# Decode attention with cached keys and values: TensorE's value products as a loop, and the spreading mask in PSUM

## The chip, the cores and the metric

The kernel runs on one NeuronCore of a Trainium2 chip. A core has TensorE (matrix products, called PE in the profile, with its weight loads as PEld), VectorE (DVE), ScalarE (ACT), GpSimd (POOL) and SyncE (SP, which here only issues transfers), and 16 DMA engines that move data between HBM and the on-chip memory SBUF. TensorE writes to PSUM, which VectorE and ScalarE can also read. The engines run apart from one another and wait on semaphores.

The metric is the time of one execution in microseconds, as the median of several runs. All numbers below in us are from one profiled execution, unless the runs are named.

## The reference

One decode step of a transformer block with batch 4, width 512, 32 heads of 128, and 4096 cached positions, all in float32:

```python
mod = (_silu(c) @ w_mod).reshape(c.shape[0], 6, 1, -1)   # sa, ca, ga, sb, cb, gb
h = _layernorm(x) * (1 + ca) + sa
q = h @ wq                                               # 4 x 32 heads x 128
scores = einsum("bhqd,bhkd->bhqk", q, k_cache) * (Dh ** -0.5)
o = einsum("bhqk,bhkd->bhqd", softmax(scores), v_cache)
x = x + ga * (o @ wo)
h = _layernorm(x) * (1 + cb) + sb
x = x + gb * (silu(h @ w1) @ w2)
```

The two caches are 4 x 32 x 4096 x 128 floats each, 268 MB; together with the weights 567 MB are read once.

## The kernel before

The attention is cut into 32 tiles; tile `n` is one batch row and four heads. Its keys `k` (8.4 MB) and values `v` (8.4 MB) are loaded whole: partition `32 h + p` of `k` holds 128 consecutive positions of head `h`, 64 KB. There are two buffers for `k` (`kt[n % 2]`) and one for `v` (`vt`), so that the load of `v` for tile `n + 1` can be issued only when TensorE has read the values of tile `n`, and the load of `k` for tile `n + 2` stands behind it in SyncE's queue.

A tile's work, in `tile(n)` and `values(n)`:

- **Products with the query.** VectorE multiplies positions 0 to 47 by the query, which ScalarE has copied to PSUM (`qload`). GpSimd multiplies positions 48 to 127 in three pieces (`CUTS`).
- **Sums.** VectorE adds up the products along the 128 elements of a head (`scores`), first for positions 0 to 79 (`NA = 80`), later for 80 to 103 and 104 to 127.
- **Softmax in two halves.** `ownmax` takes the maximum of a head's 32 partitions, ScalarE takes the exponential of a half.
- **Spread.** `spread` writes the exponentials of a half into `pz`, once for each of four heads, multiplied by `mask`, a 128 x 4 table that is 1 where the partition belongs to the head and 0 elsewhere. So one TensorE product serves four heads. It is one VectorE instruction for a half: 320 elements in a partition for the first half and 192 for the second.
- **Value products.** `pv` multiplies `pz` by `v`, 20 products for the first half into one PSUM bank, 12 for the second into another, with one product for the sums of the exponentials (`fps`) between. VectorE and ScalarE join the halves into `o`, and four small products and a copy bring it into `oz`.

After tile 31 come the projection with `wo` (`regroup`, `project`), the layer norm and the two products with `w1` and `w2`; the loads of these weights stand behind the last `v` in SyncE's queue.

Instructions are recorded by the class `Plan` in program order; it works out which semaphores each must wait for, and leaves out a wait that an earlier one implies. Each engine then executes its own instructions in that order. TensorE's stream begins at a label of its own. Instructions recorded while `pl.loop` is set, which is so in `values(n)` for tiles 0 to 30, carry the tile and their place in it. Where `LOOP` is false they are written out one after the other, 37 products for each tile. Each float32 product shows in the profile as two matmuls and two weight loads.

Of the kernel before, what the change touches and what calls it, by code (L numbers as in the profile page):

```python
# [6 lines left out]
AF = mybir.ActivationFunctionType  # L7
# [1 line left out]
AX = mybir.AxisListType  # L9
ET = mybir.EngineType  # L10
PE = [ET.PE]
LOOP = False
SLOT = 16


# [25 lines left out]
class Plan:  # L41
# [108 lines left out]
    def run(self, end):  # L150
# [11 lines left out]
        with nc.body("pe_main", valid_engines=PE):  # L162
            done = False
            for o in self.ops:
                if o.eng != "PE":
                    continue
                if o.loop and LOOP:
                    if not done:
# [16 lines left out]
def build(nc, x, kc, vc, wq, wo, w1, w2, c, wm, out):  # L185
    P = 128
# [3 lines left out]
    G = 4  # L190
    W = P // G
    HP = 4
# [4 lines left out]
    JJ = 4  # L197
# [13 lines left out]
    def sb(name, *shape, at=None):  # L211
        size = 4
        for s in shape:
            size *= s
        if at is None:
            at = base[0]
            base[0] += -(-size // 32) * 32
            assert base[0] <= nc.sbuf_usable_end, (name, base[0])
        return nc.alloc_sbuf_tensor_at(name, [P, *shape], F32, offset=at)
# [10 lines left out]
    bank = [nc.alloc_psum_tensor(f"ps{i}", [P, 512], F32) for i in range(8)]  # L230
    dsem = {}

    def dma(dst, src, tag, eng="SP"):
        if tag not in dsem:
            dsem[tag] = nc.alloc_semaphore("d_" + tag)
        s = dsem[tag]
        e = pl.eng[eng]
        return pl.op(eng, lambda: e.dma_start(dst, src), [], [dst], sem=s)  # L238

    def dve(f, reads, writes):  # L240
        return pl.op("DVE", f, reads, writes)

    def act(f, reads, writes):
        return pl.op("ACT", f, reads, writes)
# [14 lines left out]
    def tt(eng, o, a, b, op=ALU.mult):  # L259
        e, q = (V, dve) if eng == "DVE" else (GP, pool)  # L260
        return q(lambda: e.tensor_tensor(o, a, b, op=op), [a, b], [o])  # L261
# [10 lines left out]
    def actv(o, a, fn, scale=1.0, bias=None, accum=None):  # L272
        kw = {"scale": scale}
        reads, writes = [a], [o]
        if not isinstance(scale, float):
            reads.append(scale)
        if bias is not None:
            kw["bias"] = bias
            if not isinstance(bias, float):
                reads.append(bias)  # L280
        if accum is not None:
            kw["accum_out"] = accum
            writes.append(accum)
        return act(lambda: A.activation(o, a, fn, **kw), reads, writes)  # L284

    def bc(a, dim, n):
        a = a.unsqueeze(dim)
        shape = list(a.shape)
        shape[dim] = n
        return a.to_broadcast(shape)  # L290
# [4 lines left out]
    mask = sb("mask", G)  # L295
# [71 lines left out]
    def vload(n, *cuts):  # L367
        t, b = divmod(n, B)
        src = vc[b, HP * t : HP * (t + 1)].rearrange("h (p j) d -> (h p) j d", p=W)
        cuts = cuts or (0, NJ)  # L370
        for i, (lo, hi) in enumerate(zip(cuts, cuts[1:])):
            tag = "C" if len(cuts) == 2 else f"v{i}"
            dma(vt[:, lo:hi, :], src[:, lo:hi, :], tag)
# [83 lines left out]
    def qexpand(t):  # L457
        j, g = divmod(t, G)
        ps = bank[2 + t % 2]
        for i in range(HP):  # L460
            mm(
                ps[W * i : W * (i + 1), :], mask[:, g : g + 1].to_broadcast([P, W]),
                E[:, HP * j + i, :, :].rearrange("p b d -> p (b d)"), True, True,
            )
        actv(qw[:, t, :], ps[:, :], AF.Copy)
# [10 lines left out]
    for t in range(1, NT):  # L476
        qexpand(t)
    vload(0)
    for i in (2, 3):
        dve(lambda i=i: V.memset(bank[i][:, :], 0.0), [], [bank[i][:, :]])  # L480

    ev = ea.rearrange("p (g j) -> p g j", j=JJ)
# [7 lines left out]
    def spread(lo, hi):  # L490
        g0, g1 = lo // JJ, hi // JJ
        w = pz[:, g0:g1, :, :]
        tt("DVE", w, bc(ev[:, g0:g1, :], 2, HP), bc(bc(mask[:, :], 1, g1 - g0), 3, JJ))

    def ownmax(h, src, col):
        rm = sc[:, col : col + 1]
# [16 lines left out]
    def tile(n):  # L513
        t, b = divmod(n, B)
        k = kt[n % 2]
        tt("DVE", k[:, :ND, :], k[:, :ND, :], bc(bank[n % 2][:, :Dh], 1, ND))
        for lo, hi in zip(CUTS, CUTS[1:]):
            tt("POOL", k[:, lo:hi, :], k[:, lo:hi, :], bc(qview(n), 1, hi - lo))
        scores(n, (0, ND))
        scores(n, (ND, NA))  # L520
        ownmax(0, sc[:, :NA], NJ)
        actv(ea[:, :NA], sc[:, :NA], AF.Exp, bias=nm[:, 0:1], accum=rs[:, 0:1])
        spread(0, NA)
        for lo, hi in zip(CUTS[1:], CUTS[2:]):
            scores(n, (lo, hi))
        ownmax(1, sc[:, NA : NJ + 1], NJ + 1)
        actv(ea[:, NA:], sc[:, NA:NJ], AF.Exp, bias=nm[:, 1:2], accum=rs[:, 1:2])
        actv(X[:, 1:2], nm[:, 0:1], AF.Exp, scale=-1.0, bias=nm[:, 1:2])
        spread(NA, NJ)
        stt(X[:, 0:1], rs[:, 0:1], X[:, 1:2], rs[:, 1:2], ALU.mult, ALU.add)  # L530
        if n + 1 < N:
            qload(n + 1)
# [130 lines left out]
```

## Time and profile before

| What | Value |
|---|---|
| Median of 3 runs | 1330.38 us (1329.06 to 1332.26) |
| The profiled execution, its own time | 1325.98 us |
| Its span, first to last instruction | 1324.6 us |
| Granted TensorE clock, mean | 0.650 |
| Busy: TensorE, VectorE, GpSimd, ScalarE | 402.1, 984.4, 710.3, 83.8 us |
| HBM read | 567.30 MB, 428 GB/s over the span |
| DMA queue of the loads (q1) | 99.4% of 16 engines over the span |

An engine's share of busy time says how much of the span it worked, not whether the end waited for it. In the timeline a row gives the start, the length, the engine, the line, the operation with its output and inputs, the shape, how many instructions are merged in the row, and in brackets how long the engine idled before it and what ended that. In the tables by window, a row gives the stretch, its length, each engine's busy time with its number of instructions, the granted TensorE clock, the DMA engines' share and the rate. The DMA queue called "instruction" carries the engines' program code.

### The profile page before, as it was taken

To read this page: it belongs to the slowest core of one execution; us is meant where nothing else is said; L and a number is where in the kernel's file an instruction comes from. 1 tells how busy PE (TensorE), PEld (TensorE's weight loads), DVE (VectorE), ACT (ScalarE), POOL (GpSimd) and SP (SyncE) were. 2 spreads that over 40 slices of the span, in tenths; PEclk is the share of its full clock that TensorE was granted. 3 is DMA by queue.
4 is the path that set the end of the run, shared out by engine and by line. 5 is a ranking of instruction groups with operands and counts; after the bars stand their busy time and mean duration, and the time that the engine had idled before them with its cause. 6 is when DMAs were issued, how large, how long until landed. Compare 5 with 4: busy or idle time off the path is not lost.

```text
span 1324.6 us, 7211 instructions
## 1 busy us (share of the span) xinstructions
PE 402.1 (30%) x3032; PEld 122.9 (9%) x3032; DVE 984.4 (74%) x582; ACT 83.8 (6%) x289; POOL 710.3 (54%) x104
## 2 busy tenths in 40 slices
PE   2433212333311333322133332223333212333346
PEld 1100000000000000000000000000000000000014
DVE  1378877777887777788777778777778877777881
ACT  1200000000000000000000000000000000000001
POOL 0345665444666544566644456655445665444750
PEclk9766566666556666655666665566666566666577
DMA  9999999999999999999999999999999999999998
GB/s 412 442 414 439 440 424 434 418 440 422 438 437 432 429 432 426 440 433 434 433 426 435 436 434 430 433 428 431 434 424 438 433 424 436 432 431 430 424 423 344
DMA packets 12125, 567.78 MB, mean 429 GB/s; under 512 B 1292, under 2 KB 1340, under 8 KB 2108
## 3 DMA queue, kind: packets, MB, share of 16 engines
q1 hardware_dynamic: 12052, 567.29, 99.4%
q8 instruction: 24, 0.39, 0.1%
q14 instruction: 9, 0.07, 0.0%
q10 hardware_dynamic: 40, 0.02, 0.0%
HBM read 567.30 MB, written 0.01 MB: 428 GB/s over the span
## 4 chain that ended last, share of the span: by engine, by line
DMA 55%; DVE 36%; PE 6%; ACT 1%; issue 1%; SPq 1%; POOL 0%; another core or an unknown queue 0%
DMA k<-in_A_k_cache_dram 49%; DVE sc L270 22%; DVE k L261 8%; PE ps L252 6%; DVE pz L261 5%; DMA wot<-in_A_wo_dram 3%; DMA wqt<-in_A_wq_dram 3%; ACT sc L284 1%; DVE rt L499 1%; SPq L238 1%; DVE nm L269 0%; POOL E L261 0%; DVE hidT L402 0%; DVE hid L265 0%
## 5 line engine op out<-in xcount | busy, mean ns | idle before, releaser
L261 POOL TENSOR_TENSOR k<-k,qw 128x3072 f32<-128x3072 f32 (+1 forms) x96 | 705.8, 7380 | 521.6 <-DMA k<-in_A_k_cache_dram 521.6
L252 PE MATMUL ps<-v,pz 128*16 128x512 f32 x2048 | 312.1, 752 | 854.0 <-DVE pz L261 854.0
L270 DVE TENSOR_REDUCE sc<-k 128x24 f32<-128x3072 f32 (+2 forms) x128 | 559.3, 4409 | 1.1
L261 DVE TENSOR_TENSOR k<-k,ps 128x6144 f32<-128x6144 f32 x32 | 209.7, 6554 | 126.1 <-DMA k<-in_A_k_cache_dram 126.1
L252 PEld LDWEIGHTS ps<-v,pz 128*16 128x16 f32 x2048 | 57.7, 113 | 1051.3 <-DVE pz L261 887.4
L261 DVE TENSOR_TENSOR pz<-sc,mask 128x320 f32<-128x320 f32 x64 | 127.6, 1994 | 32.5 <-ACT sc L284 32.5
L284 ACT ACTIVATE sc<-sc,nm 128x80 f32<-128x80 f32 x64 | 22.3, 348 | 1015.4 <-DVE nm L269 1015.4
L265 DVE SCALAR_TENSOR_TENSOR o<-ps,fr,o 128x512 f32<-128x512 f32 x32 | 24.0, 750 | 52.7 <-PE ps L252 52.7
L252 PE MATMUL ps<-sel,o 128*128 128x4 f32 x256 | 33.8, 255 | 27.9 <-DVE o L265 27.9
L538 DVE RECIPROCAL fr<-ps 128x1 f32<-128x1 f32 x32 | 5.4, 168 | 42.5 <-PE ps L252 42.5
L252 PEld LDWEIGHTS ps<-sel,o 128*128 128x128 f32 x256 | 31.0, 191 | 59.9 <-DVE o L265 59.9
L261 POOL TENSOR_TENSOR E<-qs,sel 128x2048 f32<-128x2048 f32 x1 | 3.6, 3640 | 45.5 <-ACT qs L284 45.5
L284 ACT ACTIVATE o<-ps,fr 128x512 f32<-128x512 f32 x32 | 22.0, 687 | 60.8 <-DVE fr L265 60.8
L270 DVE TENSOR_REDUCE sc<-sc 128x1 f32<-128x80 f32 x64 | 14.1, 220 | 2.2
L499 DVE STREAM_TRANSPOSE rt<-sc 128x32 f32<-128x32 f32 x64 | 13.5, 212 | 2.2
L252 PE MATMUL ps<-wmt,csT 128*32 128x256 f32 (+1 forms) x64 | 8.3, 697 | 18.2 <-DMA wmt<-in_w_mod_dram 18.2
L284 ACT ACTIVATE oz<-ps 128x4 f32<-128x4 f32 (+2 forms) x40 | 7.4, 197 | 97.5 <-PE ps L252 97.5
L269 DVE TENSOR_REDUCE nm<-rt 128x1 f32<-128x32 f32 x64 | 11.9, 186 | 2.2
L261 DVE TENSOR_TENSOR E<-qs,sel 128x2048 f32<-128x2048 f32 x1 | 2.3, 2291 | 13.6 <-ACT qs L284 13.6
L252 PE MATMUL ps<-X,selp 128*128 128x2 f32 x64 | 12.3, 262 | 0.0
L252 PEld LDWEIGHTS ps<-X,selp 128*128 128x128 f32 x64 | 9.5, 188 | 27.3 <-DVE X L265 27.3
L284 ACT ACTIVATION_READ_ACCUMULATOR sc<-sc,nm 128x1 f32 x64 | 11.9, 186 | 0.0
(62 smaller groups left out, 121.2 us busy)
## 6 DMA issues: line engine op xcount, KB each, us to landing
wmt<-in_w_mod_dram SPq DMA_DIRECT2D x1, 6144.0 KB, 17.3
k<-in_A_k_cache_dram SPq DMA_DIRECT2D x1, 5120.0 KB, 35.9
v<-in_A_v_cache_dram SPq DMA_DIRECT2D x1, 5120.0 KB, 21.0
wot<-in_A_wo_dram SPq DMA_DIRECT2D x1, 4096.0 KB, 33.9
k<-in_A_k_cache_dram SPq DMA_DIRECT2D x1, 3072.0 KB, 42.8
v<-in_A_v_cache_dram SPq DMA_DIRECT2D x1, 3072.0 KB, 24.3
wot<-in_A_wo_dram SPq DMA_DIRECT2D x1, 2048.0 KB, 38.4
wot<-in_A_wo_dram SPq DMA_DIRECT2D x2, 1024.0 KB, 42.0
```

Of the source, the lines that this page charges most:

```text
L238: return pl.op(eng, lambda: e.dma_start(dst, src), [], [dst], sem=s)
L252: lambda: nc.tensor.matmul(o, lhsT, rhs, start=start, stop=stop, skip_group_check=True),
L261: return q(lambda: e.tensor_tensor(o, a, b, op=op), [a, b], [o])
L265: return dve(lambda: V.scalar_tensor_tensor(o, a, s, b, op0=op0, op1=op1), reads, [o])
L269: return dve(lambda: V.tensor_reduce(o, a, axis=AX.X, op=op, negate=True), [a], [o])
L270: return dve(lambda: V.tensor_reduce(o, a, axis=AX.X, op=op), [a], [o])
L284: return act(lambda: A.activation(o, a, fn, **kw), reads, writes)
L499: dve(lambda: V.transpose(rt[:, h, :], a), [rm], [rt[:, h, :]])
L538: dve(lambda: V.reciprocal(fr[:, 0:1], fps[:, 0:1]), [fps[:, 0:1]], [fr[:, 0:1]])
```

## The change

Two things are changed.

- `LOOP` becomes true. TensorE's value products of tiles 0 to 30 are no longer written out 31 times; `Plan.run` writes those of one tile as the body of a loop with the tile number in a register, and the semaphore values that the body waits for are computed from it (a base and a slope for each). The loop's head is placed at slot 16 of a block of code. Tile 31 and everything behind it is written out as before.
- ScalarE copies `mask` once, ahead of the tiles, into four columns of PSUM bank 7, and `spread` reads it there. Before, both inputs of the spread lay in SBUF.

```diff
-LOOP = False
+LOOP = True
...
     vload(0)
+    actv(bank[7][:, P : P + G], mask[:, :], AF.Copy)
     for i in (2, 3):
...
     def spread(lo, hi):
         g0, g1 = lo // JJ, hi // JJ
         w = pz[:, g0:g1, :, :]
-        tt("DVE", w, bc(ev[:, g0:g1, :], 2, HP), bc(bc(mask[:, :], 1, g1 - g0), 3, JJ))
+        tt("DVE", w, bc(ev[:, g0:g1, :], 2, HP), bc(bc(bank[7][:, P : P + G], 1, g1 - g0), 3, JJ))
```

TensorE's stream behind the set-up products, before: one tile's products and the first row of the next tile's, with the semaphores that each row waits for (`d_C` is the load of `v`, `s_DVE` counts VectorE's instructions; x19 merges equal rows).

```order
L252 MATMUL ps<-v,pz 16x512 [waits d_C,s_DVE]
L252 MATMUL ps<-v,pz 16x512 x19
L252 MATMUL ps<-v,pz 16x512 [waits s_DVE]
L252 MATMUL ps<-v,pz 16x512 x3
L252 MATMUL ps<-X,selp 128x2 [waits s_DVE]
L252 MATMUL ps<-v,pz 16x512 x8
L252 MATMUL ps<-sel,o 128x4 [waits s_DVE]
L252 MATMUL ps<-sel,o 128x4 x3
L252 MATMUL ps<-v,pz 16x512 [waits d_C,s_DVE]
```

The same place now, from the body's second row to the branch that closes it; ahead of these rows stand the counter's start, a branch to the head, and the body's first product, which waits for `d_C` and `s_DVE` as before. The rows stand once and are run 31 times.

```order
L252 MATMUL ps<-v,pz 16x512 x19
L174 REGISTER_ALU
L252 MATMUL ps<-v,pz 16x512 [waits s_DVE]
L252 MATMUL ps<-v,pz 16x512 x3
L174 REGISTER_ALU
L252 MATMUL ps<-X,selp 128x2 [waits s_DVE]
L252 MATMUL ps<-v,pz 16x512 x8
L174 REGISTER_ALU
L252 MATMUL ps<-sel,o 128x4 [waits s_DVE]
L252 MATMUL ps<-sel,o 128x4 x3
L171 REGISTER_ALU
L171 COMPARE_AND_BRANCH
```

The products keep their order and wait for the same semaphores. New are one register operation ahead of each group that waits for VectorE, and a step of the counter and a branch at the end. On VectorE no instruction moves; the two spreads of a tile read `ps` in place of `mask`:

```order
L269 TENSOR_REDUCE nm<-rt 128x1 [waits s_DVE]
L261 TENSOR_TENSOR pz<-sc,ps 128x320 [waits s_ACT]
L270 TENSOR_REDUCE sc<-k_85 128x24 [waits s_POOL] x2
L270 TENSOR_REDUCE sc<-sc 128x1 [waits s_DVE]
L500 STREAM_TRANSPOSE rt<-sc 128x32 [waits s_DVE]
L269 TENSOR_REDUCE nm<-rt 128x1 [waits s_DVE]
L261 TENSOR_TENSOR pz<-sc,ps 128x192 [waits s_ACT]
```

The spreads wait for ScalarE's exponential as before, and for nothing more.

## The prediction

> **What bounds the kernel now.** I read the page's slices and queues first, then the tiles one by one by windows, then one tile's timeline, and the forms of the spread last.
>
> ```profile
> span 1324.6 us, 7211 instructions
> PE 402.1 (30%) x3032; PEld 122.9 (9%) x3032; DVE 984.4 (74%) x582; ACT 83.8 (6%) x289; POOL 710.3 (54%) x104
> ...
> DMA  9999999999999999999999999999999999999998
> ...
> q1 hardware_dynamic: 12052, 567.29, 99.4%
> q8 instruction: 24, 0.39, 0.1%
> ```
>
> No engine is near its span, but the queue of the loads takes 99.4% of 16 DMA engines. So a tile should last as long as its 16.8 MB do, whatever VectorE does. The windows below run from VectorE's first instruction of a tile, which waits for its keys, to that of the next. These are 7 of the 30 rows for tiles 0 to 29, the first and the last among them; after the clock, the last two columns are the DMA share and GB/s.
>
> ```profile
> 58.10:96.96 38.86, 11.14 (x74) 3.06 (x74) 30.54 (x18) 2.10 (x8) 22.05 (x3) 0.63 1.00 432
> ...
> 213.82:252.52 38.70, 11.61 (x74) 3.11 (x74) 30.48 (x17) 2.10 (x8) 22.05 (x3) 0.63 0.99 423
> ...
> 563.58:602.28 38.70, 11.02 (x74) 3.08 (x74) 30.47 (x17) 2.10 (x8) 22.06 (x3) 0.63 1.00 434
> 602.28:640.98 38.70, 10.45 (x74) 3.02 (x74) 30.48 (x17) 2.09 (x8) 22.05 (x3) 0.63 1.00 434
> ...
> 679.68:718.39 38.71, 11.00 (x74) 3.08 (x74) 30.47 (x17) 2.09 (x8) 22.05 (x3) 0.63 1.00 433
> 718.39:757.61 39.22, 10.43 (x74) 2.98 (x74) 30.47 (x18) 2.10 (x8) 22.05 (x3) 0.63 1.01 435
> ...
> 1185.90:1224.60 38.70, 10.48 (x74) 3.01 (x74) 30.47 (x17) 2.10 (x8) 22.05 (x3) 0.63 1.00 429
> ```
>
> The column after VectorE's 30.5 us of 38.7 is ScalarE's. Many tiles last 38.70 us to the hundredth: a floor that the transfers set, 16.78 MB at 434 GB/s. From 58.10 to 1224.60 are 1166.50 us; 30 floors of 38.70 make 1161.0. So 5.5 us are above the floor in these tiles. What makes a tile longer? The DMA view of the long tile and of the one at 563.58:
>
> ```profile
> DMA packets 293, 17.06 MB, mean 435 GB/s; under 512 B 32, under 2 KB 32, under 8 KB 32
> ...
> q1 hardware_dynamic: 292, 17.04, 100.4%
> q8 instruction: 1, 0.02, 0.2%
> ```
>
> ```profile
> DMA packets 288, 16.78 MB, mean 434 GB/s; under 512 B 32, under 2 KB 32, under 8 KB 32
> ...
> q1 hardware_dynamic: 288, 16.78, 100.3%
> ```
>
> The long tile holds one packet of program code on q8, the short one none. I asked this view for all 30 windows: 18 hold a q8 packet, and their lengths are together 5.1 us above 18 floors (0.28 us each, between 0.00 and 0.83); the 12 without one are together 0.4 us above. q8 is TensorE's code: its 6064 instructions in the page, at 64 bytes each as an estimate from 0.39 MB / 6064, fill the queue's bytes. One packet is 0.39 MB / 24 = 16 KB; at 434 / 16 = 27 GB/s that is 0.60 us of one DMA engine. A tile has 288 - 32 = 256 large packets, 16 for each engine, back to back; VectorE waits for the last engine. So a fetch that meets the engine which is last costs up to 0.60 us, and one that meets an engine with room costs nothing (602.28:640.98 holds one too). That fits 0.00 to 0.60; the three tiles above it have something else besides.
>
> The chain of waits hides this, and the waits of SyncE do too:
>
> ```profile
> DMA 55%; DVE 36%; PE 6%; ACT 1%; issue 1%; SPq 1%; POOL 0%; another core or an unknown queue 0%
> ```
>
> ```profile
> SPq L238 <- PE ps L252: 1226.1, 34, 44.3
> ```
>
> The chain goes from a load back to its issue, and from there over TensorE to VectorE, since `v` may be issued only when TensorE has read the last `v`. But an issued load still stands behind the one that runs. One tile shows how far ahead it is:
>
> ```profile
> 602.33 22.05 POOL L261 TENSOR_TENSOR k<-k,qw 128x4096 f32<-128x4096 f32 x3 [16.65 <-DMA k<-in_A_k_cache_dram]
> ...
> 621.01 3.72 DVE L261 TENSOR_TENSOR pz<-sc,mask 128x320 f32<-128x320 f32 x1 [0.52 <-ACT sc L284]
> 624.65 6.60 DVE L270 TENSOR_REDUCE sc<-k 128x24 f32<-128x3072 f32 x2
> 624.78 0.15 PEld L252 LDWEIGHTS ps<-v,pz 128*16 128x16 f32 x8 [25.58 <-DVE pz L261]
> ...
> 633.85 0.30 PEld L252 LDWEIGHTS ps<-X,selp 128*128 128x128 f32 x2 [0.85 <-DVE X L265]
> ...
> 636.13 0.33 SPq L238 DMA_DIRECT2D v<-in_A_v_cache_dram  x1
> ...
> 640.98 6.55 DVE L261 TENSOR_TENSOR k<-k,ps 128x6144 f32<-128x6144 f32 x1 [4.09 <-DMA k<-in_A_k_cache_dram]
> ```
>
> `v` is issued 4.85 us before the next keys have landed (640.98 - 636.13). In the tile at 213.82 it was issued at 249.13:
>
> ```profile
> 249.13 0.33 SPq L238 DMA_DIRECT2D v<-in_A_v_cache_dram  x1
> ```
>
> That is 3.39 us ahead of 252.52, 1.46 us less than usual, and that tile still took 38.70. So this wait doesn't bind.
>
> **The change part by part.** *The mask in PSUM.* The forms apart:
>
> ```profile
> L261 DVE TENSOR_TENSOR k<-k,ps 128x6144 f32<-128x6144 f32 x32 | 209.7, 6554 | 126.1 <-DMA k<-in_A_k_cache_dram 126.1
> L270 DVE TENSOR_REDUCE sc<-k 128x48 f32<-128x6144 f32 x32 | 209.7, 6553 | 1.1
> L261 DVE TENSOR_TENSOR pz<-sc,mask 128x320 f32<-128x320 f32 x32 | 116.1, 3629 | 16.7 <-ACT sc L284 16.7
> L261 DVE TENSOR_TENSOR pz<-sc,mask 128x192 f32<-128x192 f32 x32 | 11.5, 359 | 15.8 <-ACT sc L284 15.8
> L284 ACT ACTIVATE ps<-qw 128x128 f32<-128x128 f32 x32 | 8.3, 258 | 0.0
> ```
>
> 320 elements take ten times as long as 192. The larger spread begins while GpSimd multiplies its last piece and ends at 624.73, 0.35 us after GpSimd does (602.33 + 22.05 = 624.38); the smaller runs when GpSimd is done. So the spread with both inputs in SBUF stands still until GpSimd ends. The products `k<-k,ps`, with one input in SBUF and one in PSUM, run wholly beside GpSimd and take no longer than the sum over the same elements (6554 against 6553 ns), which has one input. With the mask in PSUM I take the small spread's 359 ns and 128 elements more, at (6554 - 359) / (6144 - 192) = 1.04 ns each: 0.49 us. VectorE saves 3.72 - 0.49 = 3.2 us a tile, some 100 us in all. The sums behind it wait for GpSimd's last piece at 624.38: the first of the two would end at 621.50 + 6.60 / 2 = 624.80, after that, so the whole 3.2 us reach TensorE and the issue of `v`: about 8.0 us ahead of the landing instead of 4.85. In time that is worth little: where 1.46 us less lead cost nothing, 3.2 us more gain nothing. Bounds: 0, and the 0.4 us of the tiles without a fetch; I take 0.2. VectorE then waits 3.2 us longer for keys. The added copy is at most one `ps<-qw` row, 0.26 us, in the set-up, where the load of the first keys is what is waited for: 0.
>
> *The loop.* Code for 30 tiles' products is no longer fetched. The fetches in tiles 0 to 29 cost 5.1 us; one at the entry may stay (0.28). The trace shows no loop, so from both sides: the best is the floor in all 30 tiles, -5.5 us with the mask's part in it; at the other end it fetches a block again at each turn, below. I take 4.8 us, since the one body of 37 products is 37 / 1516 of all products, 0.6 of a packet.
>
> *What the loop adds.* Three register operations, a step and a branch in each turn. No row shows one. Two of them stand ahead of products on the way to the issue of `v`. The nearest rows on this way are TensorE's waits: the 0.85 us ahead of the weights of `X`. Twice that, 1.7 us a tile, is less than the 3.2 us that the mask frees, so it would move an issue that isn't waited for; the lower bound is 0. The branch falls in the 25.58 us in which TensorE idles between tiles. Cost: 0. The cover for it is the lead of `v`; were it gone, every us would count 30 times.
>
> *The end.* The projection and the last products are bound by `wo`, `w1`, `w2` behind the last `v` in the same queue, and their code is fetched as before: 0.
>
> Sum: -4.8 - 0.2 = -5.0 us. The profiled execution took 1325.98, so 1321.0; it lies 4.4 us below the median of the runs, and nothing of the profile says where those have the rest. The same step from 1330.38 gives 1325.4.
>
> **The rivals.** *The loop fetches at each turn (slower).* [...] No run here shows a branch yet. As a mechanism of this kernel: one packet in each of 31 turns at 0.28 us is 8.7 in place of 5.1 us, +3.6 - 0.2: 1333.8; two packets a turn give 1342.5. It decides from 18 packets in 30 tiles on. For it: no row. Against: the body is 0.6 of a packet and stands at one place in a block, and with more lead of `v` the engines that weren't hit can go on. Chance 0.07.
>
> *No change.* The link of packet and length is another's doing, say both follow from the tile's phase, or the lost time returns at the end, where `w1` and `w2` have waits of their own. Against: twelve tiles without a packet average 0.03 us above the floor. For: the runs lie 4.4 us above the profiled one for reasons unseen, and may drown 5. Time 1330. Chance 0.23.
>
> *More than forecast.* The runs' 4.4 us are of the same kind, fetches that meet the last engine more often (18 x 0.60 = 10.8 at most): 1330.38 - 5.0 - 4.4 = 1321.0. Chance 0.10.
>
> *The spread stays blocked,* if the exponentials' read alone stands behind GpSimd. Against: `k<-k,ps`. VectorE's 100 us don't come, and the time hardly differs: 1325.6. Chance 0.05, within the forecast's side.
>
> **How the numbers follow.** The measurement tells about 0.2%, 2.7 us, from no change. The forecast, 1325.4, has 0.55; with the blocked spread and the larger gain 0.70 lie on the faster side, 0.23 within, 0.07 slower. The range goes from the larger gain, a little below 1321, to no change, 1331.
>
> **What the profile would show.** Right: q8 falls from 24 packets to 5 or 8, none in the tiles; tiles at 38.70 throughout; the 128x320 spread near 490 ns; VectorE's busy time near 884 us; `v` issued some 8 us ahead of the landing; GB/s up by a third of a per cent. Wrong: q8 at 30 or more; tiles above 38.70 with no packet in them; a spread at 3.6 us; or `v` issued no earlier, if the loop's registers ate what the mask frees.

## The result, and the profile after

| | Median (range), us | Kernel before in the same comparison | Ratio, 95% interval |
|---|---|---|---|
| Changed kernel | 1322.67 (1322.42 to 1324.0), 4 runs | 1331.2 (1329.06 to 1332.26), 4 runs | 0.994 (0.9923 to 0.9957) |

The change made the kernel 0.6% faster, 2.7 us below the forecast of 1325.4 and inside its range. The runs also lie closer together: 1.6 us apart where the kernel before has 3.2 in as many runs.

The page of the profiled execution (1322.78 us) shows what the edits were to do to the code and to VectorE:

```profile
span 1321.4 us, 7400 instructions
PE 400.7 (30%) x3032; PEld 120.4 (9%) x3032; DVE 883.7 (67%) x582; ACT 83.9 (6%) x290; POOL 711.0 (54%) x104
...
q1 hardware_dynamic: 12052, 567.29, 99.4%
q8 instruction: 6, 0.10, 0.0%
q14 instruction: 9, 0.07, 0.0%
```

q8, TensorE's code, fell from 24 packets to 6; VectorE's busy time from 984.4 to 883.7 us. q14 carries code that isn't TensorE's, 9 packets of 8 KB, as before; the experiments will show that VectorE's is among it. The spreads by form (busy us and mean ns, then the idle time ahead of them):

```profile
L261 DVE TENSOR_TENSOR pz<-sc,ps 128x320 f32<-128x320 f32 x32 | 15.6, 487 | 16.7 <-ACT sc L284 16.7
L261 DVE TENSOR_TENSOR pz<-sc,ps 128x192 f32<-128x192 f32 x32 | 11.3, 354 | 15.8 <-ACT sc L284 15.8
```

The large spread takes 487 ns where it took 3629. In the timeline of one tile it runs in the middle of GpSimd's products, which end at 561.92 + 22.08 = 584.00, and `v` is issued 600.57 - 592.48 = 8.09 us before VectorE starts on the next keys:

```profile
561.92 22.08 POOL L261 TENSOR_TENSOR k<-k,qw 128x4096 f32<-128x4096 f32 x3 [16.62 <-DMA k<-in_A_k_cache_dram]
...
580.60 0.49 DVE L261 TENSOR_TENSOR pz<-sc,ps 128x320 f32<-128x320 f32 x1 [0.52 <-ACT sc L284]
...
592.48 0.33 SPq L238 DMA_DIRECT2D v<-in_A_v_cache_dram  x1
...
600.57 6.55 DVE L261 TENSOR_TENSOR k<-k,ps 128x6144 f32<-128x6144 f32 x1 [7.33 <-DMA k<-in_A_k_cache_dram]
```

But the tiles are not all at the floor. The windows are cut as in the prediction; the first row is tiles 0 to 29 as one stretch:

```profile
57.90:1222.83 1164.93, 333.30 (x2220) 91.99 (x2220) 817.12 (x511) 62.86 (x240) 662.33 (x90) 0.63 1.00 433
```

```profile
561.87:600.57 38.70, 10.59 (x74) 3.02 (x74) 27.24 (x17) 2.10 (x8) 22.08 (x3) 0.63 1.00 434
...
639.28:678.92 39.64, 11.13 (x74) 3.09 (x74) 27.23 (x17) 2.10 (x8) 22.07 (x3) 0.63 0.99 428
...
1183.18:1222.83 39.65, 10.54 (x74) 3.00 (x74) 27.23 (x18) 2.10 (x8) 22.07 (x3) 0.63 1.01 437
```

1164.93 - 1161.0 leaves 3.9 us above the floor, where the prediction left 0.5. Only five tiles are over 38.75, and four of them carry 3.7 of the 3.9 us, 0.85 to 0.96 each. Each of the four holds a packet that the prediction did not count, one of q14. The DMA view of the tile at 639.28:

```profile
q1 hardware_dynamic: 291, 16.97, 99.0%
q14 instruction: 1, 0.01, 0.1%
```

Against the profile of before the span is 3.2 us shorter: 1.6 in the tiles, 1.4 behind them, 0.2 ahead. The medians differ by 8.5. So the profile of before was a quick execution of its kernel, and the next section asks where the others lose their time.

### The profile page after: what moved, and what is told of

Read it like the earlier page. It is cut to its first block, busy times and chain, and to the rows that moved or that the text cites. A ratio compares the mean times of both kernels' runs of the same rounds, so it can differ in the third digit from the quotient of the medians.

```text
span 1321.4 us, 7400 instructions
## 1 busy us (share of the span) xinstructions
PE 400.7 (30%) x3032; PEld 120.4 (9%) x3032; DVE 883.7 (67%) x582; ACT 83.9 (6%) x290; POOL 711.0 (54%) x104
## 3 DMA queue, kind: packets, MB, share of 16 engines
q1 hardware_dynamic: 12052, 567.29, 99.4%
## 4 chain that ended last, share of the span: by engine, by line
DMA 60%; DVE 32%; PE 5%; ACT 1%; SPq 1%; issue 1%; POOL 0%
DMA k<-in_A_k_cache_dram 55%; DVE sc L270 22%; DVE k L261 8%; PE ps L252 5%; DMA wqt<-in_A_wq_dram 3%; DMA w2t<-in_B_w_dram 2%; ACT sc L284 1%; DVE pz L261 1%; SPq L238 1%; DVE rt L500 1%; DVE nm L269 0%; POOL E L261 0%; DVE o L265 0%; ACT qs L284 0%; DVE y L261 0%
## 5 line engine op out<-in xcount | busy, mean ns | idle before, releaser
L261 DVE TENSOR_TENSOR pz<-sc,ps 128x320 f32<-128x320 f32 x64 | 26.9, 421 | 32.5 <-ACT sc L284 32.5
L252 PE MATMUL ps<-wqt,hT 128*32 128x512 f32 x64 | 9.4, 752 | 11.1 <-DMA wqt<-in_A_wq_dram 11.1
```

The costliest lines, as they stand in the source:

```text
L252: lambda: nc.tensor.matmul(o, lhsT, rhs, start=start, stop=stop, skip_group_check=True),
```

## The experiments

In all of them the kernel before ran beside on the same chip, its medians between 1327.07 and 1328.95 us (11 to 30 runs a comparison). "Above the floor" is the time of tiles 0 to 29 less 1161.0 us; "lead" is the time from `v`'s issue to VectorE's start on the next keys.

**The kernel before once more.** No edit.

> The kernel before, unchanged, for a second profile of it and for the spread of its runs. Its first profiled execution took 1325.98 us, the median of its runs 1331.2. If the runs' 5 us more are of the same kind as the 5.5 us above the floor (engines hit by code fetches, late issues of v), this profile has tiles 0 to 29 together 8 to 11 us above 30 x 38.70. If they lie outside the tiles, the tiles stand at 5 to 6 us above the floor again whatever the time. Ratio 1.000 +- 0.002.

1331.26 us (1325.81 to 1335.34), ratio 1.0019 (1.0003 to 1.0036). So the same kernel stands 2.3 us from itself, and a difference of that size between kernels means little. This profiled execution took 1330.96 us. All its tiles, and two of them:

```profile
58.07:1230.19 1172.12, 334.37 (x2220) 92.37 (x2220) 914.30 (x510) 62.85 (x240) 661.55 (x90) 0.63 1.00 430
```

```profile
485.72:526.27 40.55, 11.09 (x74) 3.08 (x74) 30.48 (x17) 2.10 (x8) 22.06 (x3) 0.63 1.01 433
...
1151.53:1191.50 39.97, 10.99 (x74) 3.08 (x74) 30.47 (x17) 2.10 (x8) 22.05 (x3) 0.63 1.02 441
```

11.1 us above the floor instead of 5.5, with the same 24 packets of q8. The 5 us by which the runs exceed the first profile are lost in the tiles. SyncE's rows ahead of the two:

```profile
482.26 0.33 SPq L238 DMA_DIRECT2D v<-in_A_v_cache_dram  x1
...
1147.96 0.33 SPq L238 DMA_DIRECT2D v<-in_A_v_cache_dram  x1
```

Here `v` went out 3.46 us ahead of 485.72 and 3.57 us ahead of 1151.53, and the tiles behind took 1.85 and 1.27 us more than the floor. The first holds a packet of q14, though none of q8; the second holds no packet of code at all.

**The loop alone,** from the kernel before:

```diff
-LOOP = False
+LOOP = True
```

> Loop, mask left in SBUF. Theory A (the prediction's): the loop alone is worth nearly all, since it takes away 18 fetches of TensorE's code: 7.5 to 8.5 us less than before, tiles as in the changed kernel, v issued some 4.9 us ahead of the landing. Theory B (lead): what counts is how far ahead v is issued; with 4.9 us an engine that was not hit must wait for v and loses what it is ahead, so hits add up. With few hits left the loop alone still gains 6 to 8, and the mask alone gains as much. Theory C (the mask does it): loop alone 0 to 2 us.

1325.88 us (1323.26 to 1330.48), ratio 0.9976 (0.9961 to 0.999): 3.1 us off 1328.95. The profiled execution was the quickest of the twelve. The gain lies between what the three theories gave (7.5 to 8.5, 6 to 8 and 0 to 2), and not far above the 2.3 us by which the kernel before differs from itself.

```profile
57.76:1222.83 1165.07, 328.26 (x2220) 93.00 (x2220) 914.29 (x511) 62.86 (x240) 661.54 (x90) 0.64 1.00 433
```

Six packets on q8, but 4.1 us above the floor. Only one tile has a late issue, at 35.43 us into it where the median is 33.85; the tile behind that one took 39.95 us and holds no packet of code.

**The mask alone,** from the changed kernel:

```diff
-LOOP = True
+LOOP = False
```

> Mask in PSUM, no loop. Theory A: 0.2 us less than before at most, 24 q8 packets, tiles 0 to 29 still 5 us or more above the floor. Theory B: 6 to 8 us less than before, though all q8 packets are still there: with 8.1 us of lead each engine keeps what it is ahead, a hit of some 0.5 us on one of sixteen engines costs nothing unless it meets the last one again; the tiles stand 3.9 to 5 us above the floor, most of that in four tiles with a q14 packet. Theory C: 7 to 8.5 us less.

1322.81 us (1322.35 to 1323.27), ratio 0.9955 (0.9937 to 0.9973): 6.1 us off 1328.95, as much as the whole change in a comparison of the same kind (below), with all of TensorE's code fetched:

```profile
q8 instruction: 24, 0.39, 0.1%
```

```profile
58.09:1222.36 1164.27, 327.49 (x2220) 96.57 (x2220) 817.26 (x511) 62.88 (x240) 662.23 (x90) 0.63 1.00 433
```

So with the longer lead the loop adds nothing that these runs show: 17 packets more in the tiles, and no more time above the floor (3.3 us; 3.9 with the loop). Where those 3.3 us lie differs. Two tiles that hold only a packet of q8 have 1.17 and 0.78 of them, and the four that were 0.85 to 0.96 too long in the changed kernel are here 1.2 too long together.

**More code for VectorE.** 18 memsets of one element each in a tile, from the changed kernel; their values are not used.

```diff
+        for i in range(18):
+            a = bank[7][:, 256 + i : 257 + i]
+            dve(lambda a=a: V.memset(a, 0.0), [], [a])
```

> The changed kernel with 18 more one-element VectorE instructions in each tile, behind the tile's last VectorE work, where VectorE idles for some 7 us. In the changed kernel four tiles with a q14 packet are 0.85 to 0.96 us long above the floor, 3.7 us of the 3.9. If these packets are VectorE's code and always meet the same DMA engine, their number doubles and the kernel takes 3.5 to 4.5 us more than the changed one: 4 to 5 us less than before. If they are another engine's code, four such tiles remain and the time is that of the changed kernel, 8.5 us less than before.

1326.94 us (1326.66 to 1327.76), ratio 0.9986 (0.9975 to 0.9996), 4.0 to 4.3 above the changed kernel's 1322.98 and 1322.67. VectorE works only 0.4 us a tile longer, which its wait for keys covers. What grew is q14, from 9 packets to 13, so VectorE's code is there, and eight tiles that hold one are longer:

```profile
563.64:602.34 38.70, 10.21 (x74) 2.96 (x74) 27.63 (x35) 2.10 (x8) 22.08 (x3) 0.63 1.00 434
602.34:642.04 39.70, 11.33 (x74) 3.14 (x74) 27.64 (x36) 2.10 (x8) 22.08 (x3) 0.63 1.02 441
```

```profile
q1 hardware_dynamic: 299, 17.50, 101.9%
q14 instruction: 1, 0.01, 0.1%
```

The second fence is the DMA view of 602.34:642.04. Seven such tiles at 39.65 to 39.70 and one at 39.18 make 7.2 of the 7.85 us above the floor (1168.85 us for the 30), 3.9 more than in the changed kernel.

**VectorE's tiles as a loop too.** Its instructions for tiles 0 to 29 become the body of a loop of its own, two tiles a turn, with its head at slot 0 of a block (the recording and the fit of semaphore values are done for VectorE as for TensorE). Two places of the edit; for VectorE, `slot` is 0:

```diff
+                            with nc.Fori(mine[0], max(mine) + 1, engines=[E], head_slot={E: slot}) as i:
...
+        if n < 30 and n % 2 == 0:
+            pl.dloop = (n // 2, 0)
```

> The changed kernel with VectorE's instructions of tiles 0 to 29 a loop as well, two tiles in a turn. Theory B: the q14 packets that stretched four tiles by 0.85 to 0.96 us are VectorE's code (18 more instructions a tile doubled them to eight) and vanish but for one or two; tiles 0 to 29 stand under 0.5 us above 30 x 38.70, and the time is 3.5 us below the changed kernel's, near 1319. VectorE's register operations cost at most 2 us of the 8 us by which v is issued ahead. Rival: register operations ahead of every VectorE instruction take 5 us a tile or more, v comes late, and the kernel is as slow as the one before or slower.

1320.35 us (1320.06 to 1321.76), ratio 0.9936 (0.9915 to 0.9956). The tiles behind the first are all at the floor, 29 x 38.70 = 1122.3:

```profile
97.49:1219.86 1122.37, 319.13 (x2146) 89.11 (x2146) 789.92 (x494) 60.75 (x232) 640.24 (x87) 0.63 1.00 434
```

The first tile starts 5 us late: the changed kernel's starts at 57.90. VectorE idles ahead of it for nothing that the profile names ("issue"), and in 60:63 lies one packet of q14:

```profile
63.24 6.55 DVE L270 TENSOR_TENSOR k<-k,ps 128x6144 f32<-128x6144 f32 x1 [6.80 <-issue]
```

```profile
q14 instruction: 1, 0.01, 0.7%
```

**The same without the jump to slot 0,** so that the body stands right behind the code ahead of it:

```diff
-                            with nc.Fori(mine[0], max(mine) + 1, engines=[E], head_slot={E: slot}) as i:
+                            with nc.Fori(mine[0], max(mine) + 1, engines=[E], head_slot={E: slot} if eng == "PE" else None) as i:
```

> The VectorE loop again, without a set place for its head in a block of code: it stands right behind the code ahead of it. With the set place VectorE stood idle for 6.8 us at the loop's entry, after a branch, with a q14 packet in it, and the first tile began at 63.24 in place of 57.9; the tiles caught up but for 0.9 us. Theory: the first tile begins at 58 again, all 30 tiles at the floor, 0.9 us less than with the set place: 1319.4, 3.3 us below the changed kernel. Rival: the body now lies across a boundary of two blocks and a block is fetched at each turn: 15 or more q14 packets, which always meet the same DMA engine at 0.9 us each: 12 us more.

1319.61 us (1319.19 to 1320.7), ratio 0.9938 (0.9921 to 0.9955), the quickest of all these kernels.

```profile
57.69:1219.16 1161.47, 331.26 (x2220) 92.25 (x2220) 817.12 (x511) 62.87 (x240) 662.27 (x90) 0.63 1.00 433
```

0.5 us above the floor in 30 tiles. q14 has 5 packets left; those of the four long tiles are gone. The stall came with the jump to the loop's head, not with the turns.

**The mask with `v` issued as late as before.** From the mask alone; a sum is done twice, 3.34 us of VectorE's time a tile between the second half's sums and its softmax. The second result is not used.

```diff
+        red(bank[7][:, 256:280], k[:, CUTS[1] : CUTS[2], :])
```

> Mask in PSUM, no loop, and one sum over 24 positions done a second time by VectorE (3.34 us a tile, its result not used), so that v is issued 4.8 us ahead of the landing as in the kernel before, though no spread waits for GpSimd. Theory B (what the mask gives is lead): all of the mask's 6 us are lost again, 0 +- 2 us against the kernel before, runs spread over 5 us or more, engines bunched. Rival (the spread's standstill beside GpSimd itself costs, or the mask's gain has another way): 4 to 6 us less than before stay.

1343.16 us (1343.02 to 1349.34), ratio 1.0109 (1.0085 to 1.0132). The profiled execution is the slowest of the five, 1349.34. The price overshot its purpose: the median lead is 3.98 us (2.25 to 7.70) and not 4.8, since TensorE's products of the second half ran slower in tiles like the one below. In windows of TensorE alone (busy time, granted clock, DMA share, rate), the 26 matmuls after the second spread, in this kernel and below it in the one before:

```profile
641.99:648.00 6.01, 5.97 (x26) 0.51 0.88 382
```

```profile
632.87:636.12 3.25, 3.20 (x26) 1.00 0.89 383
```

So `v` was issued at 648.02, 2.30 us ahead of 650.32. The tiles before and after that point:

```profile
611.52:650.32 38.80, 13.12 (x74) 3.45 (x74) 30.40 (x18) 2.10 (x8) 22.08 (x3) 0.62 1.02 433
650.32:690.49 40.17, 12.87 (x74) 3.38 (x74) 30.41 (x19) 2.10 (x8) 22.08 (x3) 0.64 0.97 418
```

The tile that follows the late issue is the longer one. 25.0 us stand above the floor: a mask in PSUM with a shorter lead loses. No spread waits for GpSimd in this kernel, so it isn't the end of that standstill by itself that gains.

**Later still.** From the changed kernel, two such sums, 6.7 us a tile:

```diff
+        red(bank[7][:, 256:280], k[:, CUTS[1] : CUTS[2], :])
+        red(bank[7][:, 288:312], k[:, CUTS[2] : CUTS[3], :])
```

> Loop and mask, and two sums over 24 positions done a second time (6.7 us a tile, results not used): v issued at 37.3 us into the tile, some 1.4 us ahead of the landing. Theory B: the first packet of v comes some 2.4 us after its issue, so v starts at 39.7, the keys after it land 38.7 later, and two tiles take 39.7 + 38.7 + 0.5 = 78.9: 39.45 a tile, 23 us more than floor, near 1342. Rival (a lead of 1 us suffices, since it is above 0): 1323 to 1326.

1393.35 us (1391.21 to 1396.95), ratio 1.0491 (1.0464 to 1.0518). Median lead 1.10 us, 1217.21 us for the 30 tiles, 56.2 above the floor: 40.57 a tile. The expectation was too low: it had `v` issued 37.3 us into a tile, and the median is 39.04.

**The changed kernel once more.** No edit.

> The changed kernel as it is, for a direct comparison on this chip with the VectorE loop: 0.994 of the kernel before, 1322 to 1324 us, runs within 2 us of one another.

1322.98 us (1322.34 to 1323.84), ratio 0.9951 (0.9933 to 0.9969).

**Only the order.** From the kernel before, without the loop and with the mask in SBUF; the sums of positions 80 to 103 move ahead of the first half's softmax, so that the large spread comes when GpSimd is nearly done:

```diff
         scores(n, (ND, NA))
+        scores(n, CUTS[1:3])
...
-        for lo, hi in zip(CUTS[1:], CUTS[2:]):
-            scores(n, (lo, hi))
+        scores(n, CUTS[2:4])
```

> The kernel before, with the mask in SBUF and no loop; VectorE sums positions 80 to 103 ahead of the first half's softmax and not behind it. So the larger spread begins at 22.07 us into the tile, when GpSimd ends (22.1), and stands still for no more than 0.4 us. v is issued near 32.3 us into the tile, 6.4 us ahead of the landing: TensorE's first half starts at 22.5 as before and the second behind it at 29. Theory B (lead alone is what the mask gave): 4 to 6 us less than before, runs within 2 us, with all 24 q8 packets. Rival (the mask's place itself, or VectorE's standstill, is what counts, and 1.5 us of lead nothing, as the prediction had it): 0 +- 1 us.

1322.54 us (1322.34 to 1322.85), ratio 0.9959 (0.9942 to 0.9975): the time of the changed kernel, with neither of its parts, and 4.5 us off the 1327.07 measured beside it. One tile of the timeline:

```profile
584.79 0.59 DVE L261 TENSOR_TENSOR pz<-sc,mask 128x320 f32<-128x320 f32 x1 [0.52 <-ACT sc L284]
...
594.39 0.33 SPq L238 DMA_DIRECT2D v<-in_A_v_cache_dram  x1
...
601.64 6.55 DVE L261 TENSOR_TENSOR k<-k,ps 128x6144 f32<-128x6144 f32 x1 [6.50 <-DMA k<-in_A_k_cache_dram]
```

The spread from SBUF takes 0.59 us there, `v` goes out 7.25 us ahead (median 6.67), and the tiles are 3.3 us above the floor with all 24 packets of q8 fetched. This edit ends the spread's standstill too; it was the late mask above that told the standstill from the lead.

**Where the 16 engines stand.** Each load ends with one small packet on every DMA engine (the 32 under 512 B in the DMA view of a tile, which has two loads), so the trace holds 16 landing times for the keys of each tile. The trace doesn't name the engines; it gives their order. The table has the first landing and the last, in us against a grid of 38.70 from the first tile's start; a figure that doesn't move means that nothing is lost at that place. The engine that lands first is called the foremost.

| Kernel | Median lead | behind tile 1 | tile 11 | tile 17 | tile 23 |
|---|---|---|---|---|---|
| before, first profile | 4.86 | -2.23 / -0.31 | -0.08 / 1.73 | 0.09 / 2.44 | 1.52 / 3.65 |
| before, again | 4.86 | -2.22 / -0.50 | 0.26 / 3.27 | 2.93 / 6.40 | 5.50 / 7.98 |
| loop alone | 4.86 | -1.66 / -0.17 | -1.26 / 0.75 | 0.52 / 2.15 | 0.53 / 2.56 |
| mask alone | 8.09 | -2.48 / -0.49 | -2.45 / -0.14 | -2.44 / 1.18 | -2.44 / 1.78 |
| order only | 6.67 | -2.44 / -0.50 | -2.42 / -0.19 | -2.41 / 1.07 | -2.41 / 1.79 |
| changed | 8.09 | -2.32 / -0.54 | -2.30 / 0.36 | -2.29 / 1.34 | -2.29 / 2.34 |
| both loops, the quicker | 8.09 | -2.10 / -0.11 | -2.03 / -0.09 | -1.98 / -0.08 | -1.94 / -0.08 |

With the long lead the foremost engine keeps its place to 0.16 us over these 22 tiles. With 4.86 us it falls back by 2.2 to 7.7 us and stays 1.5 to 3.5 us ahead of the last. In the changed kernel the last engine alone slips, by about 1 us at each packet in the four long tiles, while the second to last stays between -0.60 and -0.49; in the kernel with both loops nothing slips.

Behind tile 23, where the last engine has slipped far, the foremost moves too: in this profile of the changed kernel it falls back from -2.29 to -1.24 by tile 29. In the second profile of that kernel, where no issue is late, it stands at -2.14 there. With more code for VectorE the last engine slips further, and the foremost begins to move at tile 18.

**What an engine needs.** Where `v` has long been issued when an engine has its keys, the engine's first packet of `v` follows at once and takes 2.42 us, as nearly all of 64 KB do. Behind the latest issues engines stand idle. In the tile at 213.82 of the first profile the first packets of `v` start 0.96 us after the issue, and those of the idle engines take 2.75 to 3.3 us. Six engines had their keys before that, and the foremost falls back by 1.39 us in the next tile. With `v` later still all 16 ran dry, as behind the issues at 422.67 and 544.48; there the first packets start 0.96 us after the issue too, and the second ones after 3.9 to 4.5 us, as if `v` had flowed from 1.5 to 2.1 us on. The 2.4 us of that run's expectation are too long for an idle engine.

In the changed kernel's profile the foremost keeps its place to 0.07 us from one tile to the next, except behind two issues, 1.54 and 1.87 us before it had its keys; there it falls back by 0.35 and 0.66. In the kernel before, with the usual lead, it has them 2.4 to 2.5 us after the issue in the early tiles. Behind the three late issues of the first profile it falls back by 1.39, 0.18 and 1.13 us, 2.7 of the 4.8 that it loses from tile 0 to tile 29.

**Where the late issues come from.** In three tiles of the first profile, the one at 213.82 among them, `v` went out 35.15 to 35.39 us into the tile and not 33.85. TensorE's 26 matmuls of the second half took 4.5 to 4.8 us there at a granted clock of 0.66 to 0.69, and 3.2 at 1.00 in all others that stand apart from the first half. Two rows of the tile at 213.82, and then the same 16 matmuls in the tile at 602.28:

```profile
244.40 1.05 PE L252 MATMUL ps<-v,pz 128*16 128x512 f32 x8 [2.22 <-DVE pz L261]
...
245.70 3.40 PE L252 MATMUL ps<-v,pz 128*16 128x512 f32 x16
```

```profile
634.16 1.91 PE L252 MATMUL ps<-v,pz 128*16 128x512 f32 x16
```

TensorE had idled 2.13 to 2.26 us ahead of these three, and 2.07 at most ahead of the others.

## Why the prediction was right, and which step failed

**The bound and the unit of cost held.** The tiles are bound by their transfers, 38.70 us each, and program code on the same DMA engines lengthens them (39.22 us with one packet of q8 in the kernel before, 39.55 to 39.66 with one of q14 in the changed one). More of VectorE's code made the kernel slower by 4.2 us; with both engines' tiles as loops 30 tiles took 1161.47. The sum's -5.0 us stand against -5.7 (the later comparison: 1322.98 against 1328.71) to -8.5. But its two terms were wrong, and their errors partly cancelled; that the sum came out near was luck.

**The step that failed is "where 1.46 us less lead cost nothing, 3.2 us more gain nothing".** The mask was put at 0.2 us; alone it gives 6.1. The row it rested on, 213.82:252.52 at 38.70, shows one tile, and the cost came behind it. The next two rows of that profile:

```profile
252.52:291.64 39.12, 11.24 (x74) 3.06 (x74) 30.48 (x17) 2.10 (x8) 22.06 (x3) 0.63 0.99 429
291.64:330.50 38.86, 10.46 (x74) 3.02 (x74) 30.49 (x18) 2.09 (x8) 22.06 (x3) 0.63 1.01 432
```

The first of them holds a packet of q8, so the two causes can't be told apart by it. The tiles at 1151.53 of the second profile and at 523.40 of the loop alone hold no code and are 1.27 and 1.25 us long behind a late issue. Not every late issue shows at once: of eight in the three profiles with the usual lead, three have a tile of 38.56 to 38.72 behind them.

The lead was measured against VectorE's wait, which the last engine ends. The foremost engine is done 2 us earlier, and then needs work. In the second tile of the first profile `v` is issued at 130.81 and the foremost has its keys at 133.27, 2.46 us later. By the packets that is just enough, and an issue that is 1.5 us late makes it wait. So the wait binds at the foremost engines though it doesn't at the last. What follows is shown too: with a longer lead, by either of two quite different edits, the foremost loses nothing over 22 tiles; with a shorter one the foremost are dragged along, and the time rises. It is 1322.5 and 1322.8 us at 6.7 and 8.1 us of lead, 1325.9 to 1331 at 4.9, 1343 to 1349 at 4.0 and 1393 at 1.1. For the last one the chain nearly closes by an estimate: `v` goes out 39.04 us into a tile, 1.5 to 2.1 until it flows, 38.70 for its values and the keys behind them, and 0.5 to VectorE's start make 79.7 to 80.3 for two tiles, 39.9 to 40.2 a tile where 40.57 were measured.

**The loop's 4.8 us were mis-sized too.** Alone it gives 3.1, with the mask nothing. The fetches do lengthen tiles in the kernel before, as the DMA view of the long tile showed (39.22 us with one packet of q8). But there the engines have little in hand, and part of the 5.1 us that stood beside the fetches may belong to the late issues, which the runs don't separate in that profile. Given the lead, most of 18 packets cost no time; the engines other than the last have up to 2 us to spare (mask alone: the foremost at -2.4 in all of the table). They aren't quite free, since two tiles still lost 2.0 us to them; but without them the last engine lost as much to VectorE's packets instead. So the terms were not independent: either part removes some of the same loss, and the sum of the parts alone, 9.2, is not the 5.7 of both in a comparison of the same kind.

**"Tiles at 38.70 throughout" was wrong** by the four tiles with a packet of q14. The prediction counted q8 alone in each window; the "something else" that it noted in three tiles was not followed up. q14 has 9 packets in either kernel; in the changed one those of VectorE's code set the tiles' excess almost alone, and with VectorE's loop they are gone, which was worth 3.1 to 3.4 us more (1319.61 against 1322.67 and 1322.98).

**The rivals.** That the loop fetches at each turn: no. q8 has 6 packets, and the kernel with VectorE's loop has none in 29 tiles; VectorE's own loop began 14 turns there, with 3 packets of q14. Only at the entry by a jump did VectorE stand, 6.80 us with a packet of q14 in them; the profile doesn't show that it waited for that packet. That nothing changes: no. More than forecast, since the runs' extra time is of the same kind: its 1321.0 is nearer to 1322.67 than the forecast is, though in the later comparison the gain is nearer to the forecast's. The extra time does lie in the tiles (11.1 against 5.5 us), but not in more packets, of which there are 24 in both; the engines are dragged along, and the mask, more than the loop, takes that away. That the spread stays blocked: no, 487 ns.

**Also as predicted:** the spread near 490 ns, VectorE near 884 us, `v` about 8 us ahead, q8 within 5 to 8. The loop's registers ate none of the lead (8.09 us with the loop and without it).

**Open.** Why VectorE's packets meet the same engine each time, the one that is last already, and why they cost less where TensorE's are fetched too, isn't settled. The stretch behind the tiles is 1.4 us shorter in the first profile of the change than in the first of before; in the second profile of the change it is as long as there (99.98 us), so it varies from one execution to another, and why isn't known. What lowers TensorE's clock in some tiles is open too, as the last point below says.

## What to carry to other kernels

Where a queue is as full as here (99.4% of 16 engines), ask which engine the consumer's wait speaks of: VectorE's, over 4.85 us after the issue, told of the last one, and the foremost had its keys 2.4 to 2.5 us after it. Look how far ahead of the *foremost* engine the next load is issued, and give it a few us more before anything else: moving one line gave here the time that both edits gave together. Program code came over the same 16 DMA engines as the loads (a tile with one packet of VectorE's was up to 0.96 us longer), so count the code packets of every engine in the long windows, not only of the one with the most code. And price two edits against one another before adding their gains: if both remove the same loss, the second may be worth nothing.

## What the runs showed of the hardware

- A tile with one 8 KB packet of VectorE's code was up to 0.96 us longer in the changed kernel and up to 1.0 with more code, more than the 0.60 us estimated for a 16 KB packet of TensorE's. A tile with one of TensorE's was up to 1.17 us longer with the mask alone.
- At a jump to a loop's head VectorE idled 6.80 us, where in the changed kernel it waits 1.38 for its keys; without the jump the first tile started at 57.69 instead of 63.24.
- Where DMA engines stood idle in the tile at 213.82 of the first profile, the first packets of `v` started 0.96 us after its issue at the earliest, and 12 of the 16 took 2.75 to 3.3 us for 64 KB, where the packets behind them took 2.42.
- TensorE's granted clock was 0.51 over the second half's products after 4.95 us of idle time, and 1.00 in the kernel before after 1.89: 5.97 against 3.20 us for the same 26 matmuls. The rows of the two waits, the kernel before second:

```profile
641.99 1.91 PE L252 MATMUL ps<-v,pz 128*16 128x512 f32 x8 [4.95 <-DVE pz L261]
```

```profile
632.87 1.05 PE L252 MATMUL ps<-v,pz 128*16 128x512 f32 x8 [1.89 <-DVE pz L261]
```

The idle time alone doesn't decide it: with the mask late, 3.47 us of it went before 0.65 in one tile and before 1.00 in another, and in the kernel before 25.58 us went before 0.72 over the first half's products (624.78:631.00).
